# Attention steps with a gated FFN: rest-row scores by column group, dummy products removed, and the turn of a first k fill moved into the next step

## The chip, the cores and the metric

The kernel runs on one core of a Trainium2 chip. The metric is device time in microseconds (us) of one execution; the kernel before has a median of 2300.26 us over three runs (2291.55 to 2302.47). Profiles are of one further execution each, and their times are counted from its first instruction.

TensorE (PE in the profile, its weight loads PEld) multiplies, VectorE (DVE) and ScalarE (ACT) copy and compute, GpSimd (POOL) copies and issues DMAs, and SyncE (SP) issues most of the loads. Each engine works through its instructions in the order in which they were written.

## The reference

```python
g = sigmoid((x * gate_w).sum(-1, keepdims=True))          # x: 2048 x 1024
# A: attention over segments of 32 rows; 8 memory rows pass from one segment to the next
for s in range(64):
    h = concat([mem, x[32*s:32*s+32]])                    # 40 rows x 1024
    q, k, v = (h @ W for W in (Wq, Wk, Wv))               # 32 heads of 128
    p = softmax(where(mask, q @ k.T * 128**-0.5, -1e9))   # mask: i < 8 or i >= j
    o = (p @ v) @ Wo
    mem, out[s] = o[:8], o[8:]
# B: a gated FFN of 3584, independent of A
b = gelu(x @ w_gate) * (x @ w_up) @ w_down
return g * a + (1 - g) * b
```

The 64 segments of A depend on each other through `mem` alone: 8 rows out of one step are inputs of the next. Rows and weights are bf16.

## The kernel before

**Stages.** A short start transposes x and writes it out in a layout for the steps (`xq_scr`, `xr_scr`). Then come 64 attention steps, which take up the time from about 0.1 to 1.66 ms. A projection of the remaining outputs and the FFN follow; the change does not touch them.

**Rows of a step.** Of a segment's 40 rows, a step computes on the path from memory to memory only 32: its first 24 x rows and the 8 memory rows (`NR = 24`). The last 8 x rows of a segment, the "rest" (`NB = 8`), depend on no memory in their q, k and v. Those of four segments together (32 rows, `hR`) are projected in advance in a "fill", one matrix (q, k or v) and one half of the heads at a time. `FILL` says which fills a step carries: one or two, by the step's number modulo 4: (k1, q1), (v0, q0), (v1), (k0). The first fill of a step (`f1`) runs in bank A1 in the second half of the step, the second (`f2`, in steps 0 and 1 of 4) in bank B0 at the beginning of the next step.

**What happens with a fill.** `fill_evac` (L856) lets ScalarE copy the bank into a stage buffer. For v, four POOL DMAs write it to DRAM from there. For q and k, `fill_put` (L867) follows: a "turn" (TensorE transposes four 128x128 blocks into PSUM bank TT, L673), a VectorE copy back into the same buffer in a new order (L873), and a POOL DMA to `qk_scr` (L876) on the DMA lane `fq`. A lane has one semaphore, and each DMA of a lane waits until the one before has landed. Steps four and more later read these rows back (`load_qk`, L536).

The stage buffer of a first fill is `kS`. It lies in the memory of `kT` and is also the buffer into which ScalarE copies each step's own k of the first half of the heads (`evac`, L656), ahead of that k's turn. The planner of the program (`_Prog`) derives all waits from such overlaps: a write waits for every earlier reader of the same bytes, DMAs included.

**Order.** The program is written as a walk over weight pieces: 8 pieces for each matrix and half of the heads. A step's walk is: four pieces of k (round 0), two of q, the last four of the previous step's output projection, two of q, four of v, then the rest of k, q and v of round 0, then round 1 of k, q, the output projection, v, and four more of the output projection. `plan(s)` hangs all other work on a place in this walk: `on("k", 0, 2, f)` runs f ahead of the third k piece. Within an engine that order stands.

**Between two steps.** When the first four pieces of the last output projection are through (L804), `fold(s, 0)` (L815, L816) adds the halves on VectorE into `a_bf`. `next_mem(s, 0)` has TensorE transpose it (L825) and VectorE copy the 8 memory rows into `hT` of the next step (L828), and the first k piece (L771) reads that. Where the step has a second fill, four of its pieces stand before L825 and four behind it. Where it has none, `warm` (L851) issues five and two rounds of four products of 32x512 whose result nobody reads. `fill_put` of a first fill stands ahead of the fold, at `("o", 1, 3)` (L983).

**Scores.** For a half of the heads, 16 heads lie in a 4x4 grid (j, g): g chooses a 32-row group of PSUM, j a place in its columns. `scores` makes, for every (j, g), one product of 32 query rows and one of the 8 rest rows with the 40 keys (L700), into columns 80j and 80j + 40. A mask (`mS`, L687) is added by a product beforehand. The softmax (L706 to L714) works on all 128 rows at once; its result `pAB` is transposed in blocks of 32x32 by two VectorE instructions of 256 columns (L720). `attend` multiplies with v: L729 waits for the first of the two, L737 for the second.

**Queues.** SP issues the weight loads as slots come free: a freed pair of k pieces lets SP issue the next k load (L431), and so on. POOL issues, in its order, the loads of rest rows (L536, L540), the fills' writes (L862, L876) and each step's `a_scr` write (L1004), with its own copies in between (L754, L880).

Of the kernel before, what the change touches and what calls it, by code (L numbers as in the profile page):

```python
# [8 lines left out]
ALU = mybir.AluOpType  # L9
# [201 lines left out]
def bass_gated_mix__memory_aug_recurrent_mem_tr__geglu_ffn__prompt_kernel(  # L211
# [21 lines left out]
    NB = SEG - NR  # L233
# [12 lines left out]
    with ExitStack() as es:  # L246
# [218 lines left out]
        for g in range(4):  # L465
            q = slice(32 * g, 32 * g + 32)


            pw(mS, lambda e, q=q: sel(e, mS[q, 0:NR], ALU.is_ge, NEG, 0, [[-1, NR]], 1))
            pw(mS, lambda e, q=q: sel(e, mS[q, 32:40], ALU.is_ge, NEG, -NR, [[0, NB]], 1))  # L470

            pw(mS, lambda e, q=q: sel(e, mS[q, 72:80], ALU.is_ge, NEG, 0, [[-1, NB]], 1))
# [15 lines left out]

        def tr_mem(e):
            for kc in range(KC):  # L490
                ins = e.transpose(PBV[5][:, kc * 8:(kc + 1) * 8], pm[0:8, kc * 128:(kc + 1) * 128], ident[0:8, 0:8])
            return ins
# [62 lines left out]
        op("pe", tr_mem, rd=[pm.r(), ident.r()], wr=[BK(5)])  # L555
# [135 lines left out]
        def scores(u, masked=True):  # L691
# [3 lines left out]
            def f(e):  # L695
                for n, c in ((32, 0), (8, 40)):
                    for j in range(4):
                        for g in range(4):
                            x = 8 * (4 * j + g)
                            ins = e.matmul(PB[SS][32 * g:32 * g + n, j * 80 + c:j * 80 + c + LQ],  # L700
                                           lhsT=qT[:, j, g, :] if n == 32 else qkr[:, 2 * u, x:x + 8],
                                           rhs=kT[:, j, g, :], start=False, stop=True, skip_group_check=True)
                return ins
# [15 lines left out]
            for c in (0, 256):  # L719
                op("dve", lambda e, c=c: e.transpose(tAB[:, c:c + 256], pAB[:, c:c + 256]), rd=[pAB.r(c, c + 256)], wr=[tAB.r(c, c + 256)], after=[fin])  # L720
# [126 lines left out]
        def warm(n):  # L847
            def f(e):
                for x in range(4 * n):
                    g = x % 4  # L850
                    ins = e.matmul(PB[B0][32 * g:32 * g + 32, :], lhsT=hR[:, 7, :], rhs=spare[:, g * 512:(g + 1) * 512],  # L851
                                   start=True, stop=True)
                return ins
            spare = slots[home["q", 0, 7]]
            op("pe", f, rd=[hR.r(224), spare.r()], wr=[BK(B0)])

# [11 lines left out]
        def fill_put(m, u, G, st, bank=TT):  # L868
            if m == "v":
                return  # L870
            st = stage[st]
            turn(st, bank)
            op("dve", lambda e: e.tensor_copy(st[:, :].rearrange("p (i x c) -> p x i c", i=4, x=16),  # L873
                                              PBV[bank][:, 0:512].rearrange("p (x i c) -> p x i c", x=16, i=4)), rd=[BK(bank)], wr=[st.r()])
            m4 = 3 * u if m == "q" else 1 + u
            op("pool", lambda e: e.dma_start(qk_scr[:, 4 * G:4 * G + 4, m4, :], st[:, :].rearrange("p (i y) -> p i y", i=4)),  # L876
               rd=[st.r()], wr=[("D", "qk", G, m, u)], lane="fq")
# [22 lines left out]
        def plan(s):  # L900
# [80 lines left out]
            if fl:  # L981
                on("o", 1, 0, lambda: fill_evac(*fl[0], A1, "k"))
                on("o", 1, 3, lambda: fill_put(*fl[0], "k"))  # L983
# [10 lines left out]
            on("k", 0, 0, some(f2, 4) if two else lambda: warm(5), **nx)  # L994
            on("k", 0, 0, lambda: next_mem(s, 0), **nx)
            on("k", 0, 0, some(f2, 4) if two else lambda: warm(2), **nx)
            if two:
                on("k", 0, 0, lambda: fill_evac(*fl[1], B0, ua), **nx)
# [177 lines left out]
```

## Time and profile before

| what | value |
|---|---|
| median of 3 runs | 2300.26 us |
| the profiled execution | 2308.1 us, its span 2306.3 us |
| TensorE busy over the span | 2119.9 us, 92% |
| VectorE, ScalarE, GpSimd busy | 1028.8, 541.4, 423.7 us |
| products of the steps' projections (L771) | 12288, 778.4 us busy |
| products of fills (L841) | 3072, 225.3 us busy |
| dummy products (L851) | 924, 64.6 us busy |
| scores (L700), 32 rows and 8 rows | 2048 each, 37.1 and 37.4 us busy |
| transposes (L720) | 256 of 256 columns, 98.7 us busy |
| DMA, mean over the span | 277 GB/s, of which q1 (SP) 596.58 MB of 638.34 |

How to read it: "busy" of TensorE counts modelled ends of pipelined products, so four products into four column groups overlap, and a set of four of 512 columns takes about 0.217 us of TensorE's time. The line of 40 slices has 57.7 us a slice; the steps lie in slices 3 to 28. In the timeline a row has start, length, engine, line, operation, operands and count; in brackets stands the idle time ahead of it and what ended it. A DMA's row is the time of its issue only; its landing is in another view. PEclk is the clock that was granted to TensorE, in tenths.

### The profile page before, as it was taken

Reading aid. Unit: us, or ns where it says so; the run is one execution under the profiler, and the core shown is the slowest. Engines: PE = TensorE matmul, PEld = TensorE weight load, DVE = VectorE, ACT = ScalarE, POOL = GpSimd, SP = SyncE. Lnnn points to the kernel's source line nnn. Section 1 sums busy time; section 2 is a strip of 40 time slices with the busy share of each in tenths; the row PEclk is TensorE's granted clock in tenths of the full one; section 3 lists DMA queues with packets and bytes.
Section 4 is the critical chain, followed back from the end, with each engine's and each line's share of the span. In section 5 each row is a group of like instructions: output and inputs, shape, how many; then the busy total and the mean of one; then the engine's idle time right before and its main releaser. Section 6 shows DMA issues by size and latency. Waiting matters only on the chain.

```text
span 2306.3 us, 74586 instructions
## 1 busy us (share of the span) xinstructions
PE 2119.9 (92%) x33852; PEld 1048.7 (45%) x33852; DVE 1028.8 (45%) x2440; ACT 541.4 (23%) x1111; POOL 423.7 (18%) x821
## 2 busy tenths in 40 slices
PE   4598999999999999999999999998899999999999
PEld 2244444444444444444444444444464444444444
DVE  3343444454444444544444444454316446163462
ACT  1122222222222222222222222221113123032130
POOL 4422212222222222222222222221100000000000
PEclk8799999999999999999999999999899999999999
DMA  9989999898998999999989899999964440903520
GB/s 375 354 298 327 334 341 358 321 354 320 327 330 325 340 336 316 344 325 355 332 325 354 312 331 341 317 340 324 342 204 143 150 151 10 291 20 125 172 87 19
DMA packets 237579, 638.34 MB, mean 277 GB/s; under 512 B 22440, under 2 KB 91304, under 8 KB 230480
## 3 DMA queue, kind: packets, MB, share of 16 engines
q1 hardware_dynamic: 213440, 596.58, 72.4%
q0 software_dynamic: 13888, 26.31, 3.5%
q10 hardware_dynamic: 9936, 10.69, 1.4%
q8 instruction: 266, 4.36, 0.8%
q14 instruction: 49, 0.40, 0.0%
HBM read 596.85 MB, written 36.63 MB: 275 GB/s over the span
## 4 chain that ended last, share of the span: by engine, by line
PE 70%; DMA 19%; issue 4%; DVE 4%; ACT 2%; POOL 1%; ACTq 0%; SPq 0%; POOLq 0%
PE pb L771 23%; PE pb L1077 15%; DMA sl<-in_A_Wv_dram 7%; PE pb L1131 5%; PE pb L841 5%; PE pb L804 4%; PE pb L787 4%; PE pb L673 3%; DMA qkr<-qk_scr 3%; PE pb L1027 3%; PE pb L1112 2%; PE pb L851 2%; DMA wall<-wg_scr 2%; DMA xr_scr<-xr 1%; DMA o_scr<-oRc 1%
## 5 line engine op out<-in xcount | busy, mean ns | idle before, releaser
L771 PE MATMUL pb<-sl,hT 128*32 128x512 bf16 x12288 | 778.4, 383 | 28.8 <-issue 16.9
L771 PEld LDWEIGHTS pb<-sl,hT 128*32 128x32 bf16 x12288 | 337.5, 97 | 331.6 <-issue 50.8
L841 PE MATMUL pb<-sl,hR 128*32 128x512 bf16 x3072 | 225.3, 392 | 4.1 <-issue 3.2
L1077 PE MATMUL pb<-xT,wg 128*128 128x512 bf16 x896 | 211.7, 379 | 0.7
L1077 PE MATMUL pb<-xT,wu 128*128 128x512 bf16 x896 | 211.7, 379 | 0.0
L804 PE MATMUL pb<-wall,oT 128*32 128x256 bf16 x4056 | 150.9, 275 | 22.9 <-issue 8.5
L787 PE MATMUL pb<-wall,oT 128*32 128x512 bf16 x2048 | 152.4, 387 | 17.1 <-issue 9.5
L656 ACT ACTIVATE kS<-pb 128x512 bf16<-128x512 f32 x127 | 75.8, 597 | 384.3 <-PE pb L771 364.9
L815 DVE COPY part<-pb 64x256 f32<-64x256 f32 x128 | 54.0, 422 | 247.9 <-PE pb L804 246.9
L754 POOL COPY oRc<-oT 128x128 bf16<-128x128 bf16 x128 | 96.4, 753 | 359.2 <-DVE oT L659 357.0
L1131 PE MATMUL pb<-wd,GT 128*128 128x512 bf16 x672 | 146.0, 379 | 1.7 <-DMA wd<-in_B_w_down_dram 1.7
L1085 ACT ACTIVATE s<-pb 128x512 f32<-128x512 f32 x112 | 66.8, 596 | 311.9 <-PE pb L1077 311.9
L708 ACT ACTIVATE E<-pb 128x320 bf16<-128x320 f32 x128 | 55.9, 437 | 352.9 <-DVE pb L707 352.9
L1077 PEld LDWEIGHTS pb<-xT,wg 128*128 128x128 bf16 x896 | 87.2, 98 | 108.0 <-DVE GT L1093 3.7
L1077 PEld LDWEIGHTS pb<-xT,wu 128*128 128x128 bf16 x896 | 87.7, 98 | 105.7
L804 PEld LDWEIGHTS pb<-wall,oT 128*32 128x32 bf16 x4056 | 100.6, 96 | 74.9 <-ACT oT L656 25.9
L1086 DVE SCALAR_TENSOR_TENSOR tp<-s,pb 128x512 f32<-128x512 f32 x112 | 77.0, 687 | 124.2 <-ACT s L1085 124.0
L659 DVE CAST oT<-pb 128x160 bf16<-128x160 f32 x256 | 76.5, 320 | 111.7 <-PE pb L737 111.7
L659 DVE COPY kT<-pb 128x512 bf16<-128x512 bf16 x128 | 54.4, 425 | 159.8 <-PE pb L673 159.5
L880 POOL COPY kT<-qkr 128x128 bf16<-128x128 bf16 x128 | 37.3, 291 | 466.3 <-DVE kT L659 222.6
L841 PEld LDWEIGHTS pb<-sl,hR 128*32 128x32 bf16 x3072 | 82.3, 98 | 70.7 <-issue 20.8
L1090 DVE SCALAR_TENSOR_TENSOR tp<-tp,pb 128x512 f32<-128x512 f32 x112 | 77.1, 688 | 78.6 <-ACT tp L1089 78.6
(100 smaller groups left out, 2286.8 us busy)
## 6 DMA issues: line engine op xcount, KB each, us to landing
sl<-in_A_Wv_dram SPq DMA_DIRECT2D x128, 1024.0 KB, 10.8
wall<-wg_scr SPq DMA_DIRECT2D x53, 1536.0 KB, 9.2
sl<-in_A_Wk_dram SPq DMA_DIRECT2D x64, 1024.0 KB, 5.9
sl<-in_A_Wq_dram SPq DMA_DIRECT2D x64, 1024.0 KB, 9.0
wall<-wo_scr SPq DMA_DIRECT2D x120, 512.0 KB, 6.0
wd<-in_B_w_down_dram SPq DMA_DIRECT2D x42, 1024.0 KB, 5.4
sl<-in_A_Wv_dram SPq DMA_DIRECT2D x75, 512.0 KB, 11.1
wall<-in_A_Wo_dram SPq DMA_DIRECT2D x41, 512.0 KB, 7.9
```

The lines of the kernel that those rows point to most:

```text
L656: op("act", lambda e: e.activation(o, i, ACTF.Copy), rd=rd, wr=wr)
L659: op("dve", lambda e: e.tensor_copy(o, i), rd=rd, wr=wr, after=after)
L673: ins = e.transpose(PBV[bank][:, j * 128:(j + 1) * 128], st[:, j * 128:(j + 1) * 128], ident[:, :])
L754: op("pool", lambda e: e.tensor_copy(oRc[:, :, 16 * u:16 * u + 16].rearrange("p c x -> p x c"), oT[:, :, :, 32:40].rearrange("p g j c -> p ...
L771: ins = e.matmul(PB[bk][32 * g:32 * g + 32, :], lhsT=h[:, i, :], rhs=w[:, g * 512:(g + 1) * 512], start=(n == 0), stop=(n == 7))
L787: ins = e.matmul(PB[XO][32 * g:32 * g + 32, :], lhsT=oT[:, j, x, 0:32], rhs=wall[:, na:nb + 1:nb - na, c:c + 256], start=(n == 0 and hp == 0),
L804: ins = e.matmul(PB[XO][32 * g:32 * g + 32, 256 * b:256 * b + 256], lhsT=oT[:, j, x, 0:32], rhs=w[:, c:c + 256], start=False, stop=(n % 4 ...
L841: ins = e.matmul(PB[b][32 * g:32 * g + 32, :], lhsT=h[:, k[2], :], rhs=w[:, g * 512:(g + 1) * 512], start=(n == 0), stop=(n == 7))
L1077: ins = e.matmul(PB[bk][:, 0:FB], lhsT=w[:, kc, cc:cc + 128], rhs=xT[:, :, :, kc, :].rearrange("p t i c -> p (t i) c"), start=(kc == 0), s ...
L1086: op("dve", lambda e, hg=hg, t=t: e.scalar_tensor_tensor(out=t[:, :], in0=s1[:, :], scalar=1.0, in1=hg, op0=ALU.add, op1=ALU.mult), rd=[BK ...
L1090: op("dve", lambda e, hu=hu, t=t: e.scalar_tensor_tensor(out=t[:, :], in0=t[:, :], scalar=1.0, in1=hu, op0=ALU.add, op1=ALU.mult), rd=[BK( ...
L1131: ins = e.matmul(PB[bank[2 * k + hf]][:, :], lhsT=GT[:, j, tb * 128:(tb + 1) * 128], rhs=w[:, jj, hf * 512:(hf + 1) * 512], start=(j == 0) ...
```

## The change

Four things change.

1. The 8 rest rows of the four heads of a column group are multiplied together: per group g one product of 32 rows (8 for each j) with the keys of all four j, 160 columns. Of the four blocks of each row only the one with its own j is used. For this the q rows are stored g before j (in `fill_put`). The mask for the rest keys (columns 72 to 79 of `mS`) is now needed for all 32 rows of a group; it is made once at the start from a small tile `mT`, through a TensorE transpose. 
2. The transposes of `pAB` become four of 128 columns: first the rest blocks of both halves, placed 56 columns apart, so that head j's 8 rest columns come to lie at 64j + 32; then the main blocks, which overwrite what is unused. Each of the latter waits for the rest transpose of its half.
3. `warm` goes, with both its calls.
4. `fill_put` of a first fill moves from `("o", 1, 3)` of its step, ahead of the fold, to `("k", 0, 2)` of the next step, behind L825 and two k pieces.

```diff
-            pw(mS, lambda e, q=q: sel(e, mS[q, 72:80], ALU.is_ge, NEG, 0, [[-1, NB]], 1))
...
+        mT = al("mT", [128, 16, NB])
+        pw(mT, lambda e: e.memset(mT[0:NB, :, :], 0.0), True)
+        pw(mT, lambda e: sel(e, mT[0:NB, :, :], ALU.is_ge, NEG, 0, [[0, 16], [1, NB]], -1))
...
+            e.transpose(PBV[5][:, 64:64 + NB], mT[0:NB, :, :].rearrange("p x i -> p (x i)"), ident[0:NB, 0:NB])
...
+        op("dve", lambda e: e.tensor_copy(mS[:, 72:80], PBV[5][:, 64:64 + NB]), rd=[BK(5)], wr=[mS.r(72, 80)])
...
-                for n, c in ((32, 0), (8, 40)):
-                    for j in range(4):
-                        for g in range(4):
-                            x = 8 * (4 * j + g)
-                            ins = e.matmul(PB[SS][32 * g:32 * g + n, j * 80 + c:j * 80 + c + LQ],
-                                           lhsT=qT[:, j, g, :] if n == 32 else qkr[:, 2 * u, x:x + 8],
-                                           rhs=kT[:, j, g, :], start=False, stop=True, skip_group_check=True)
+                for j in range(4):
+                    for g in range(4):
+                        ins = e.matmul(PB[SS][32 * g:32 * g + 32, j * 80:j * 80 + LQ], lhsT=qT[:, j, g, :],
+                                       rhs=kT[:, j, g, :], start=False, stop=True, skip_group_check=True)
+                for g in range(4):
+                    ins = e.matmul(PB[SS][32 * g:32 * g + 32, 0:320].rearrange("p (j c) -> p j c", j=4)[:, :, LQ:80],
+                                   lhsT=qkr[:, 2 * u, 32 * g:32 * g + 32],
+                                   rhs=kT[:, :, g, :], start=False, stop=True, skip_group_check=True)
...
-            for c in (0, 256):
-                op("dve", lambda e, c=c: e.transpose(tAB[:, c:c + 256], pAB[:, c:c + 256]), rd=[pAB.r(c, c + 256)], wr=[tAB.r(c, c + 256)], after=[fin])
+            def halves(k, w, after):
+                return [op("dve", lambda e, c=c: e.transpose(tAB[:, c + 32 * k:c + 32 * k + 4 * w].rearrange("p (j x) -> p j x", j=4)[:, :, 0:32],
+                                                             pAB[:, c:c + 256].rearrange("p (j k x) -> p j k x", j=4, k=2)[:, :, k, :]),
+                           rd=[pAB.r(c, c + 256)], wr=[tAB.r(c, c + 256)], after=[x]) for c, x in zip((0, 256), after)]
+            halves(0, 64, halves(1, 56, [fin, fin]))
...
-            op("dve", lambda e: e.tensor_copy(st[:, :].rearrange("p (i x c) -> p x i c", i=4, x=16),
-                                              PBV[bank][:, 0:512].rearrange("p (x i c) -> p x i c", x=16, i=4)), rd=[BK(bank)], wr=[st.r()])
+            to = st[:, :].rearrange("p (i g j c) -> p j g i c", i=4, g=4, j=4) if m == "q" else st[:, :].rearrange("p (i j g c) -> p j g i c", i=4, j=4, g=4)
+            op("dve", lambda e: e.tensor_copy(to, PBV[bank][:, 0:512].rearrange("p (j g i c) -> p j g i c", j=4, g=4, i=4)), rd=[BK(bank)], wr=[st.r()])
...
-                on("o", 1, 3, lambda: fill_put(*fl[0], "k"))
+                on("k", 0, 2, lambda: fill_put(*fl[0], "k"), s=s + 1)
...
-            on("k", 0, 0, some(f2, 4) if two else lambda: warm(5), **nx)
+            if two:
+                on("k", 0, 0, some(f2, 4), **nx)
             on("k", 0, 0, lambda: next_mem(s, 0), **nx)
-            on("k", 0, 0, some(f2, 4) if two else lambda: warm(2), **nx)
             if two:
+                on("k", 0, 0, some(f2, 4), **nx)
                 on("k", 0, 0, lambda: fill_evac(*fl[1], B0, ua), **nx)
```

More of the change, by code (lines that the diff above doesn't have):

```diff
@@ L554, in bass_gated_mix__memory_aug_recurrent_mem_tr__geglu_ffn__prompt_kernel @@
                 load_x(n + 3)
-        op("pe", tr_mem, rd=[pm.r(), ident.r()], wr=[BK(5)])
+        op("pe", tr_mem, rd=[pm.r(), mT.r(), ident.r()], wr=[BK(5)])
+        op("dve", lambda e: e.tensor_copy(mS[:, 72:80], PBV[5][:, 64:64 + NB]), rd=[BK(5)], wr=[mS.r(72, 80)])
         op("dve", lambda e: e.tensor_copy(memT[:, :], PBV[5][:, 0:64]), rd=[BK(5)], wr=[memT.r()])
@@ L845, in fill @@
             return out
[L847 to L855, printed above, removed]
         def fill_evac(m, u, G, b, st):
```

## The prediction

> **What bounds the kernel now.** I read the page first, then the groups of instructions by form, the waits, the timeline of two neighbouring steps, and the DMA issues of short stretches.
>
> ```profile
> PE 2119.9 (92%) x33852; PEld 1048.7 (45%) x33852; DVE 1028.8 (45%) x2440; ACT 541.4 (23%) x1111; POOL 423.7 (18%) x821
> ...
> PEclk8799999999999999999999999999899999999999
> DMA  9989999898998999999989899999964440903520
> ```
>
> Attention (slices 3 to 28) keeps both TensorE and the DMA engines nine tenths busy. Its 63 step periods, measured from one first transpose of `a_bf` (L825) to the next step's, average 24.3 us. On the timeline TensorE issues with few gaps. The idle gaps of over 60 ns between 130 and 1640 us sum to 105.5 us, of which 54.5 us (74 gaps) are "issue" and 22 us end with a weight landing. So TensorE sets the pace and DMA is close behind. DMA has one thin stretch a step, just after L825, when the loads in flight have landed and no slot is free. The windows around one step show it (stretch, length, the busy time of PE, PEld, DVE, ACT and POOL, clock, DMA share, GB/s): the share falls from 0.98 to 0.64, and is 0.93 again in the next.
>
> ```profile
> 884.50:887.80 3.30, 3.28 (x85) 1.68 (x78) 1.82 (x5) 1.09 (x3) 1.71 (x3) 1.00 0.98 402
> 887.80:890.90 3.10, 2.90 (x63) 1.73 (x67) 0.17 (x1) 0.00 (x0) 0.07 (x1) 1.00 0.64 162
> ```
>
> Around that stretch lies what the change moves. On the timeline this step's L825 stands at 887.77 and its first L771 at 888.37; the next step's, which has two fills, at 912.80 and 913.83.
>
> ```profile
> 885.94 0.40 PE L673 MATMUL pb<-ident,kS 128*128 128x128 bf16 x4
> ...
> 887.09 0.78 POOL L876 DMA_DIRECT2D qk_scr<-kS  x1 [0.67 <-DVE kS L873]
> ...
> 889.02 0.38 SPq L431 DMA_DIRECT2D sl<-in_A_Wk_dram  x1
> ...
> 893.90 0.60 ACT L656 ACTIVATE kS<-pb 128x512 bf16<-128x512 f32 x1 [8.02 <-PE pb L771]
> ...
> 894.64 0.40 PE L673 MATMUL pb<-ident,kS 128*128 128x128 bf16 x4
> ```
>
> The reader is to see one buffer, `kS`, used twice. The fill's turn (885.94) leads to a DMA that reads `kS` (887.09). Then ScalarE overwrites it with this step's k (893.90), and TensorE waits for that copy before the k turn (894.64).
>
> **The change part by part.** Phases below count from a step's L825.
>
> *The moved turn.* Of the first fills only those of k are turned, so 29 turns move (31 issues of `qk_scr<-kS` less two at the start). Each takes TensorE turn, VectorE copy and POOL's DMA along. From turn to issue is 887.09 − 885.94 = 1.15 us. The new place is after 8 k products: 0.60 + 0.43 + 0.1 (change of weights), so the turn starts near 1.1 and the DMA is issued near 2.2. With two fills L771 starts at 1.03, so it is issued near 2.7. Before, it was issued at −0.67 in both. ScalarE's copy into `kS` must wait until this DMA has landed, and TensorE stands in order behind it. What is the landing time at phase 2.2 to 2.7? No `qk_scr` DMA was issued there. The nearest POOL issues are these, each a line of another answer on a short stretch (size, then us to landing):
>
> ```profile
> qk_scr<-kS POOLq DMA_DIRECT2D x1, 128.0 KB, 3.5
> vB<-v_scr POOLq DMA_DIRECT2D x1, 64.0 KB, 6.5
> vB<-v_scr POOLq DMA_DIRECT2D x1, 64.0 KB, 5.8
> qk_scr<-0S POOLq DMA_DIRECT2D x1, 128.0 KB, 6.6
> ```
>
> The first is today's, at phase −0.67 (median over all 31: 3.8). The second and third are the only two vB loads issued as late as phase 2.2 to 2.3, after SP's Wk load had started the new burst; the fourth is at phase 5.1. A DMA issued before Wk lands in 2 to 4 us, one behind it in 5.8 to 6.9. I take 6.2 (nearest in phase); ends 3.9 and 6.8.
>
> The k turn then starts 0.05 + 0.74 after the landing (893.90 to 894.64 is 0.74): at 2.2 + 6.2 + 0.8 = 9.2, and 9.7 with two fills. Undisturbed, the mean phases of that turn (27 steps of the timeline) are 6.66 and 7.41, plus 0.44 for the fill's turn now ahead of it: 7.1 and 7.85. The stall is 2.1 and 1.85 us; I take 1.9 x 29 = **+55 us**. At 3.9 it is 0, at 6.8 about 2.5 x 29 = +72.
>
> POOL: behind the moved put stand the second fill's put (steps with two fills), which shares lane `fq` and must await the k put's landing (8.9 instead of its 5.1), a_scr, and the first `kT<-qkr` copy. That copy follows the k turn's VectorE copy, itself delayed to 10.1, so it finds POOL free. That second put lands near 15 instead of 12; its reader is ScalarE's k1 copy, then delayed to about 14, and the turn behind it to about 15.9, so it hides behind the first stall. Of SP's queue only the Wq load and those after it are issued 0.4 later.
>
> What leaves the old place: VectorE's copy stood ahead of L815. L815 starts 0.16 after the last L804 product in these steps and 0.05 in the others: −0.11 x 29 = **−3**. The 0.33 of the turn itself is paid in either place. Late weights gain time during the stall: of the 22 us of landing waits and 9 us on late ScalarE copies, 29/63 lie in these steps, and I take half: **−8** (ends 0 and −14).
>
> *Scores.* One block has 16 products 128x40 and 16 of 8 rows, 0.11 us each set; after, 4 products of 160 columns replace the second set. A 512-column set of four takes 0.217, so 160 columns 0.07 at least: 0.03 x 64 second blocks = **−2**. In the first block VectorE decides.
>
> *Transposes.* Two of 256 columns end 0.445 and 0.77 after they start.
>
> ```profile
> L720 DVE STREAM_TRANSPOSE tAB<-pAB x256: 401/424/447, 92.5 to 1650.2; 128x256 bf16<-128x256 bf16 x128
> ```
>
> In the first block L737 starts 0.058 after the second transpose's end, at the median: it is bound by it. The second follows the first by 0.325. L712 (256 columns, 425 ns) and L714 (64 columns, 219 ns) give 1.07 ns a column, so 0.275 for 256, and 0.05 is fixed. Four of half the columns cost two more: +0.10 x 63 = **+6**. At worst each waits for the one before: 4 x (0.31 + 0.034) − 0.77 = +0.6, +38 us; at best 0. The second block has 0.3 us or more of slack at L729, which hides it.
>
> *Dummy products.* 231 sets of four go (924 products, 64.6 us busy). They filled the fold's wait: L825 starts 0.057 after a_bf with fills and 0.084 with dummies; the first L771 is also awaiting hT. 31 x about 0.06 = **−2**.
>
> *Instructions.* 924 + 127 x 12 = 2448 of 33852 products go, 7.2%. If the "issue" gaps shrink alike: **−4**. The start-up changes (mT on POOL, one transpose, one small copy) are under 1 us and replace four selects.
>
> *Clock.* TensorE has eight idle gaps between 1.88 and 2.5 us in slices 3 to 28, and four of them were followed by 3.4 us at a granted 0.50. One of these, and the window behind it:
>
> ```profile
> 685.93 0.59 PE L787 MATMUL pb<-wall,oT 128*32 128x512 bf16 x5 [1.88 <-issue]
> 687.00:690.40 3.40, 3.40 (x64) 1.45 (x68) 2.13 (x6) 0.44 (x1) 0.97 (x2) 0.50 0.75 213
> ```
>
> Half clock for 3.4 us costs 1.7. For stalls about 1.9 long I take a quarter of 29: 7 x 1.7 = +12. Where the dummies stood, 1.1 + 0.45 us idle leaves a 3.4 us stretch 55% busy; the stretches that lost the clock were at most 48% busy. One or two of 31 with another wait beside: +2. Sum **+14**.
>
> Sum: 55 − 3 − 8 − 2 + 6 − 2 − 4 + 14 = +56. The profiled execution took 2308.1 us (span 2306.3), 7.8 over the median of 2300.26. So 2364 on its scale, **2356 us** on the median's.
>
> **Pages against rows.** The Trainium skill, "DMA: Bandwidth & Descriptors", section "Anatomy of one DMA — SWDGE (gpsimd) path", fits a GpSimd-issued DMA with 2.0 us plus its bytes over 436 GB/s. For 128 KB that is an estimate of 2.3 us, so no stall and rival A's time. The trace agrees only in the thin stretch, where vB landed in 2.1 at the least; the 6.5 and 5.8 above speak against it. The Trainium skill, "TensorE: Matmul & The Clock Gate", section "HAM oscillation — how this bites in real kernels", puts the loss of clock at idle gaps over about 3.4 us. By that the clock would stay, rival B's time. The 1.88 us gap above, followed by 0.50, disagrees.
>
> **Rivals.**
> - A, the put lands in time, as at its old place. The limit is 4.1 us (7.1 − 0.8 − 2.2), or 4.35 with two fills. For it: a median of 3.8. Against: the vB rows. Time: no 55, no −8, clock +2: 2308.1 − 3 − 2 + 6 − 2 − 4 + 2 = 2305, 2297 on the median's scale.
> - B, the stall comes but the clock stays: four of the eight gaps kept it. 56 − 14 = +42, 2342.
> - C, the clock is lost at nearly every stall, as at the two first (2.46 and 2.48 us): 29 x 1.7 = 49 instead of 12, +93, 2393.
> - D, faster: TensorE's instruction supply. "Issue" is its largest cause of idle time (54.5 us). If 2448 products and as many weight loads fewer end half of these gaps (−27 rather than −4), it is 23 us below A: 2274. The point from which it decides is the landing: beyond about 5 us the stall (29 us for each us) outweighs it. Against: instruction fetches come in equal blocks (266 packets, 4.36 MB), so the gaps should fall with their number, by a fourteenth.
>
> **How the numbers follow.** My forecast 0.60, B 0.13, C 0.09, A 0.12, D 0.06. A measurement here tells 0.5% (11.5 us) from no change. The forecast, B and C are slower, A mostly same: slower 0.84, same 0.09, faster 0.07. The range goes from A's 2297 to a little over C's 2393, where the 6.8 us landing (+17) and worse transposes also lie: 2296 to 2400. The likeliest case's own range is 2330 to 2385.
>
> **What will show it.** Right: `qk_scr<-kS` lands in about 6 us; a new wait of ScalarE's kS copy on it, some 55 us or more in total, and of the k turn behind it; four transposes ending 0.87 after they start instead of 0.77; some 8 more windows at 0.50; steps without a k put as long as before. Wrong: kS landing in 4 us or less (A), or transposes costing 0.4 more and L737 late in all steps.

## The result, and the profile after

The changed kernel takes 2393.14 us at the median (2383.28 to 2396.66) beside 2301.36 us of the kernel before: a ratio of 1.0396, with a 95% interval of 1.037 to 1.0422. That is 92 us slower. The prediction was 2356, in a range of 2296 to 2400. Its direction holds, and its size is short by 37 us.

The profiled execution of the changed kernel has a span of 2392.7 us, 86.4 more than before. The first fence is the page of the changed kernel: busy times, the granted clock and the DMA share by slices, and the shares of the chain that ended last.

```profile
PE 2097.4 (88%) x31393; PEld 996.2 (42%) x31393; DVE 1043.8 (44%) x2697; ACT 538.5 (23%) x1111; POOL 423.7 (18%) x819
...
PEclk8699999999999999999999999999999999999999
DMA  9989999898898988899898898989976160622530
...
PE 55%; DMA 33%; DVE 5%; ACT 3%; issue 3%; POOL 1%; ACTq 0%; SPq 0%; POOLq 0%
```

TensorE is 22.5 us less busy (the dummy products are gone) in a span that is 86 us longer, so it waits 109 us more. In the chain of before TensorE had 70% and DMA 19%; now DMA has 33%. By the clock line nothing seems lost, because a slice of 60 us hides windows of 3.4 us.

All of it lies between the steps' first transposes of `a_bf`: the 62 periods between them (not 63) sum to 1506.6 us before and 1595.0 after, +88.4. Below, "one fill" and "two fills" are the two kinds of step whose beginning now holds a fill's k turn, without and with a second fill behind it. Their mean periods rise from 23.97 to 26.12 and from 24.30 to 28.00 us. The two other kinds stay (24.47 to 24.63, 24.44 to 24.07). Here is one step with two fills on the timeline of the changed kernel, cut to the rows that matter (start, length, engine, line, tiles, idle time before it and what ended that).

```profile
954.46 0.23 PE L834 MATMUL pb<-ident,a_bf 64*128 64x64 bf16 x2
...
956.03 0.40 PE L678 MATMUL pb<-ident,kS 128*128 128x128 bf16 x4
...
956.14 0.38 SPq L431 DMA_DIRECT2D sl<-in_A_Wk_dram  x1
...
957.18 0.77 POOL L875 DMA_DIRECT2D qk_scr<-kS  x1 [3.49 <-DVE kS L873]
...
964.30 0.60 ACT L661 ACTIVATE kS<-pb 128x512 bf16<-128x512 f32 x1 [6.27 <-DMA qk_scr<-kS]
...
964.76 0.76 POOL L875 DMA_DIRECT2D qk_scr<-0S  x1 [6.81 <-DMA qk_scr<-kS]
...
964.96 0.40 PE L678 MATMUL pb<-ident,kS 128*128 128x128 bf16 x4 [2.82 <-ACT kS L661]
...
971.50 0.60 ACT L661 ACTIVATE 0S<-pb 128x512 bf16<-128x512 f32 x1 [2.48 <-DMA qk_scr<-0S]
```

Read it as three links (a "put" is the DMA of `fill_put`, the "k turn" the turn of the step's own k). The fill's turn (956.03) leads to a put at 957.18, one microsecond behind the new Wk load. ScalarE's copy over `kS` waits until the put has landed, and TensorE's k turn waits for that copy: 2.82 us idle. POOL's second put, on the same lane, also waits for that landing; it goes out at 964.76, phase 10.3 instead of 5.1, and lands so late that the copy of k1 over `0S` (971.50) waits for it in turn. The stretches of the same step (length, busy time of PE, PEld, DVE, ACT and POOL, granted clock, DMA share, GB/s) show the stall, and the window that begins 1.6 us behind its end:

```profile
961.91:964.96 3.05, 0.23 (x8) 0.01 (x1) 0.00 (x0) 0.66 (x2) 0.20 (x1) 1.00 1.03 373
966.53:969.94 3.41, 3.41 (x56) 1.60 (x56) 2.26 (x7) 0.93 (x2) 0.78 (x2) 0.50 0.99 357
```

The waits of the whole execution (total, times, longest) name the same links:

```profile
ACT kS L661 <- DMA qk_scr<-kS: 231.6, 28, 12.3
...
POOL qk_scr L875 <- DMA qk_scr<-kS: 115.2, 17, 8.3
...
PE pb L678 <- ACT kS L661: 94.3, 35, 5.9
...
ACT 0S L661 <- DMA qk_scr<-0S: 33.2, 13, 4.6
```

Between 130 and 1640 us, the granted clock fell to a half in 29 windows instead of 5 (31 and 6 if counted to the end of the steps). Of the 28 steps with a moved put, 17 have such a window behind the stall. The next table puts the longer steps together from means over some 14 steps of each kind (us, before and after):

| stretch of a step | one fill | | two fills | |
|---|---|---|---|---|
| first transpose of `a_bf` to the k turn | 6.66 → 9.82 | +3.16 | 7.41 → 10.54 | +3.13 |
| k turn to attention's first product (L729, now L738) | 5.80 → 6.68 | +0.88 | 5.77 → 6.67 | +0.90 |
| from there to the turn of k1 | 0.39 → 0.32 | −0.07 | 0.34 → 1.20 | +0.86 |
| from there to the next step | 11.16 → 9.55 | −1.61 | 10.50 → 9.76 | −0.74 |

The first row holds the stall and the 0.33 to 0.44 us of the fill's own turn, the second the half clock, the third the second put. The second row is a mean of two cases: 7.29 us in the 17 steps with a window at half clock, 5.73 in the 11 without. The last row gives some back, and not because of the stall: a version without the stall ("The wait, or the place", below) has 9.89 and 9.76 us there too. It is the old place of the turn that is gone from this row.

### The profile page after: what moved, and what is told of

Read it like the earlier page. It is cut to its first block, busy times and chain, and to the rows that moved or that the text cites. A ratio compares the mean times of both kernels' runs of the same rounds, so it can differ in the third digit from the quotient of the medians.

```text
span 2392.7 us, 69920 instructions
## 1 busy us (share of the span) xinstructions
PE 2097.4 (88%) x31393; PEld 996.2 (42%) x31393; DVE 1043.8 (44%) x2697; ACT 538.5 (23%) x1111; POOL 423.7 (18%) x819
## 4 chain that ended last, share of the span: by engine, by line
PE 55%; DMA 33%; DVE 5%; ACT 3%; issue 3%; POOL 1%; ACTq 0%; SPq 0%; POOLq 0%
PE pb L780 16%; PE pb L1077 14%; DMA qk_scr<-kS 9%; PE pb L1131 6%; DMA wall<-wg_scr 5%; PE pb L796 4%; PE pb L678 3%; DMA qkr<-qk_scr 3%; DMA wall<-wo_scr 3%; PE pb L850 3%; DMA sl<-in_A_Wv_dram 2%; PE pb L813 2%; PE pb L1027 2%; PE pb L1112 2%; DMA qk_scr<-0S 2%
## 5 line engine op out<-in xcount | busy, mean ns | idle before, releaser
L780 PE MATMUL pb<-sl,hT 128*32 128x512 bf16 x12288 | 800.6, 394 | 25.4 <-DMA sl<-in_A_Wv_dram 10.1
L780 PEld LDWEIGHTS pb<-sl,hT 128*32 128x32 bf16 x12288 | 312.9, 99 | 354.6 <-issue 50.9
L850 PE MATMUL pb<-sl,hR 128*32 128x512 bf16 x3072 | 218.5, 391 | 1.9 <-issue 1.3
L678 PE MATMUL pb<-ident,kS 128*128 128x128 bf16 x384 | 41.4, 235 | 94.3 <-ACT kS L661 94.3
L726 DVE STREAM_TRANSPOSE tAB<-pAB 128x128 bf16<-128x128 bf16 x512 | 114.0, 280 | 4.4
```

Source lines behind the costliest of these rows:

```text
L678: ins = e.transpose(PBV[bank][:, j * 128:(j + 1) * 128], st[:, j * 128:(j + 1) * 128], ident[:, :])
L726: return [op("dve", lambda e, c=c: e.transpose(tAB[:, c + 32 * k:c + 32 * k + 4 * w].rearrange("p (j x) -> p j x", j=4)[:, :, 0:32], pAB[: ...
L780: ins = e.matmul(PB[bk][32 * g:32 * g + 32, :], lhsT=h[:, i, :], rhs=w[:, g * 512:(g + 1) * 512], start=(n == 0), stop=(n == 7))
L850: ins = e.matmul(PB[b][32 * g:32 * g + 32, :], lhsT=h[:, k[2], :], rhs=w[:, g * 512:(g + 1) * 512], start=(n == 0), stop=(n == 7))
```

## The experiments

Ratios are to the kernel before, with 95% intervals. Half-clock windows are counted between 130 and 1640 us. Where dummy products are in a kernel, their result is read by nothing, and the output is the same.

### The turn alone, and all but the turn

The changed kernel with the turn back at its old place:

```
-                on("k", 0, 2, lambda: fill_put(*fl[0], "k"), s=s + 1)
+                on("o", 1, 3, lambda: fill_put(*fl[0], "k"))
```

> The changed kernel with the turn of the first k fill at its old place (ahead of the fold); dummies stay out, scores and transposes stay new. If the moved turn's DMA, which holds kS against ScalarE's copy, is the cause, nearly all of the loss goes: 2290 to 2315 us (new transposes +6 to +10, the rest about 0 or a little below). If the loss came from the dummies (clock) or from VectorE's longer chain in the scores, it stays at 2340 us or more. In the profile: no wait of the kS copy on qk_scr<-kS; half-clock windows tell whether the dummies mattered (2 to 6 if not).

Measured: 2303.31 us, ratio 1.0022 (1.0005 to 1.0038). The other way round, the kernel before with this one line of the change:

```
-                on("o", 1, 3, lambda: fill_put(*fl[0], "k"))
+                on("k", 0, 2, lambda: fill_put(*fl[0], "k"), s=s + 1)
```

> The kernel before with the moved turn alone (dummies in, old scores). If the moved turn is the cause: 2380 to 2405 us, and the wait of the kS copy on qk_scr<-kS of some 230 us as in the changed kernel. If another part is: 2295 to 2310 us. Set beside e1 it tells whether the parts add up, and whether the issue gaps of TensorE (54.5 us before, 4.4 us after) vanish with the turn or with the fewer instructions.

Measured: 2374.26 us, ratio 1.0326 (1.0306 to 1.0346), which is 6 us below the band expected. So the loss goes with the moved turn. It is worth 73 us in the old kernel (2374.26 − 2301.09, the median of before beside it) and 90 (2393.14 − 2303.31) with the rest of the change; the difference comes back further down.

### The wait, or the place

If the loss is the wait for the put, a put that holds nothing up on the way to the k turn must cost nothing. Here the turn stays where the change has it, but the copy behind it goes into the buffer of `oT`, once the output projection has read that, and the DMA leaves from there, at phase 5.0 (one fill) or 5.5 (two fills) instead of 2.2 or 2.7. The second put has its own lane.

```
-                on("k", 0, 2, lambda: fill_put(*fl[0], "k"), s=s + 1)
+                on("k", 0, 2, lambda: turn(stage["k"]) if fl[0][0] != "v" else None, s=s + 1)
...
+            if fl:
+                on("q", 0, 2, lambda: fill_put(*fl[0], "k", by="o"), **nx)
...
-                on("q", 0, 2, lambda: fill_put(*fl[1], ua, SS), **nx)
+                on("q", 0, 2, lambda: fill_put(*fl[1], ua, SS, "fq2"), **nx)
```

> The changed kernel with the moved turn where it is, but its VectorE copy and its DMA go through another buffer, the stage on oT, once the o products have read it (issued near phase 4.5 to 5), and the second put has a lane of its own. The DMA still lands late (6 to 7 us), but nothing of this step's k waits for it any more. If the loss is the wait of ScalarE's kS copy for the put, and what follows from it, the k turn starts at 7.1 to 7.9 again and the time is 2295 to 2315. If the loss lies in the moved turn itself, in its VectorE copy on the path, or in the load that the late put adds to the DMA engines, it stays above 2340.

Measured: 2301.95 us, ratio 1.0007 (0.9991 to 1.0023). The k turn starts at 7.28 (one fill) and 7.89 us (two fills) instead of 9.82 and 10.54. Of ScalarE's waits in this kernel, these two matter. The copy over `kS` waits for TensorE's products, as in the kernel before, and the put now holds another copy, that of v:

```profile
ACT kS L661 <- PE pb L780: 367.3, 61, 12.4
...
ACT vA L661 <- DMA qk_scr<-oS: 44.3, 28, 2.4
```

The put itself lands as late as ever (the line on its source, which holds all of the fills' puts; the moved ones alone have medians of 7.3 and 7.2 us):

```profile
DMA to landing us min/median/max: 5.0/7.2/8.5
```

A landing 7.2 us after the issue costs next to nothing here, for TensorE waits for that copy of v only 6.1 us in all. The place of the turn is therefore not the price; the reuse of `kS` is. Beside the kernel with the second put's own lane alone (2374.81 us, below) this run is 73 us faster. The copy and the DMA did not stay at the change's place, so what they would cost there without the reuse is not shown. This is also the only version with the moved turn that is as fast as the kernel before, and no version tried is faster than that.

### When the put lands

The put is issued at phase 2.2 (one fill) or 2.7 (two fills) and lands in 6.8 or 6.9 us; at its old place it took 3.8. Is it the time since the step began, or the Wk load that SP issued in between? This kernel issues it earlier, right behind the transposes:

```
-                on("k", 0, 2, lambda: fill_put(*fl[0], "k"), s=s + 1)
...
             on("k", 0, 0, lambda: next_mem(s, 0), **nx)
+            if fl:
+                on("k", 0, 0, lambda: fill_put(*fl[0], "k"), **nx)
```

> The changed kernel with the moved turn one place further on its way back: right behind the transposes of a_bf, ahead of the first k products, not behind eight of them. The put is then issued near phase 1.65 instead of 2.2 (2.7 with two fills). If the price of the move is the landing of the put (it lands in 6.8 us when issued at 2.2 to 2.7, behind the new burst of weight loads, and in 3.8 at phase -0.67), the landing should fall to between 3.9 and 6.3 us and the k turn should start between 6.7 and 8.8 instead of 9.8 (kind with one fill) and 10.5 (two fills): time 2305 to 2350. If any place behind the transposes costs the same, whatever the load of the DMA engines, it stays at 2370 or more.

Measured: 2329.99 us, ratio 1.0113 (1.0077 to 1.0148). The timeline of this kernel shows a step with one fill and then one with two. The put leaves at the same phase in both, 1.65:

```profile
906.07 0.38 SPq L431 DMA_DIRECT2D sl<-in_A_Wk_dram  x1
906.24 0.78 POOL L875 DMA_DIRECT2D qk_scr<-kS  x1 [2.65 <-DVE kS L873]
...
933.01 0.77 POOL L875 DMA_DIRECT2D qk_scr<-kS  x1 [2.76 <-DVE kS L873]
933.71 0.38 SPq L431 DMA_DIRECT2D sl<-in_A_Wk_dram  x1
```

The DMA issues of the two stretches (size, us to landing), in the same order:

```profile
qk_scr<-kS POOLq DMA_DIRECT2D x1, 128.0 KB, 7.7
...
qk_scr<-kS POOLq DMA_DIRECT2D x1, 128.0 KB, 2.5
```

Over 14 steps each the medians are 6.32 and 2.54 us. What differs is that the put is 0.17 us behind the 1 MB Wk load in the first and 0.70 ahead of it in the second. The packets show where the time goes. In the first step, from 907.40 to 910.20 us only SP's queue moves anything (packets, MB, share of the 16 DMA engines):

```profile
q1 hardware_dynamic: 184, 0.75, 90.5%
```

Behind the load the put's first packet starts 4.2 us after the issue at the median, ahead of it 1.35 us. It does not wait for the load's end: Wk lands at 912.04, 1.6 us after the put's packets begin. So at one and the same phase the landing takes 6.3 or 2.5 us, and it goes with the order against SP's first load; no run changes that order alone. To be a little ahead is not enough: in one early step with one fill the put left 0.26 us ahead of Wk and took 5.88 us.

In the steps with two fills the k turn now starts at 8.20 instead of 10.54, with one fill at 8.92 instead of 9.82. Part of the loss stays there, and with two fills Wk is issued 0.67 later.

### The second put

A lane of its own for the second put, the rest of the change as it is:

```
-               rd=[st.r()], wr=[("D", "qk", G, m, u)], lane="fq")
+               rd=[st.r()], wr=[("D", "qk", G, m, u)], lane=lane)
...
-                on("q", 0, 2, lambda: fill_put(*fl[1], ua, SS), **nx)
+                on("q", 0, 2, lambda: fill_put(*fl[1], ua, SS, "fq2"), **nx)
```

> The changed kernel, with the second fill's put on a DMA lane of its own, so that POOL no longer holds it until the first put has landed. If POOL's wait on qk_scr<-kS (115 us, 17 times) is what makes ScalarE's copy into 0S late (33 us) and TensorE wait about 0.9 us behind L746 in 14 steps, that wait goes and the time falls by 8 to 20 us, to 2373 to 2385 us. If the second put is hidden behind the first stall, as predicted, 2388 to 2397 us.

Measured: 2374.81 us, ratio 1.0336 (1.0296 to 1.0376), 18 us less than the changed kernel by the medians and 14 by the ratios; the two intervals touch. The waits of POOL in this kernel no longer have the first put's landing ahead of the second put (115.2 us before, above):

```profile
POOL qk_scr L875 <- DVE 0S L873: 31.9, 15, 2.6
```

The second put is issued at phase 5.50 instead of 10.22 and lands at 12.07 instead of 17.25. The row from attention's first product to the turn of k1 goes from 1.20 back to 0.32. That is 0.88 us in each of 14 steps, 12 us; the rest of the 18 is not placed.

### The half clock

The next runs fill the stall with products so that TensorE is not idle in it. First, 12 sets of four:

```
+            if FILL[(s - 1) % 4][0][0] == "k" and s > 0 and s // 4 + 1 < NG:
+                on("v", 0, 4, lambda: warm(12))
```

> The changed kernel with twelve sets of four dummy products (about 2.6 us of TensorE) ahead of the k turn in the 29 steps in which it waits for kS; nothing waits for them. The wait itself stays as long. If the loss of clock behind the stalls costs time (29 more windows of 3.4 us at 0.50, at up to 1.7 us each), most of these windows vanish and the time falls by 20 to 45 us, to 2348 to 2373 us. If later waits absorb the half clock, the time stays at 2385 to 2397 us although the windows vanish. Where a stall is shorter than 2.6 us the dummies themselves cost some tenths.

Measured: 2385.97 us, ratio 1.0376 (1.0358 to 1.0393). The half-clock windows fall from 29 to 13, but 12 sets are too many: the k turn starts 0.38 (two fills) and 0.58 us (one fill) later than without them. The row behind it is shorter: k turn to attention takes 5.71 (two fills) and 5.80 us (one fill) instead of 6.67 and 6.68. So 8 sets (the same edit with `warm(8)`):

> The changed kernel with 8 sets of dummy products (32, whose result nothing reads) in front of the k turn, where 12 sets ended 0.4 to 0.6 us behind the point from which the turn had its data. 8 sets take 2.0 us of the 2.6 us stall, so the turn should start where it starts without them (9.8 and 10.5). If the loss of clock behind the stall costs what the rows from the k turn to L738 show (6.67 us without dummies, 5.75 with 12 sets, 0.9 x 31 steps = 28 us), the time is 2360 to 2372. If 0.6 us of idle time more brings the loss of clock back, or if it is made good later in the step, 2380 to 2395.

Measured: 2408.16 us, ratio 1.0448 (1.0412 to 1.0483), outside both bands and slower than without dummies. The rows show where. With one fill the step does what was expected: k turn at 9.77, attention 5.71 later, the whole step 25.79 instead of 26.37. With two fills the second put now takes 7.57 us to land instead of 6.82, and the turn of k1 waits for it until 19.06 instead of 18.41; the step grows from 28.17 to 29.31. Why the put lands later is not shown. To take that link out, both edits together:

> The second put on its own lane and 8 sets of dummy products (whose result nothing reads) in front of the k turn, both together. With the shared lane, the 8 sets brought the rows from the k turn to L738 back from 6.67 to 5.72 us, but in the steps with two fills the second put then landed later (7.57 us after its issue instead of 6.82) and k1's copy waited for it, so the step was 1.1 us longer, not shorter. With its own lane nothing waits for the second put. If that is the whole of it, the loss of clock is worth about 0.9 to 1.2 us in each of 29 to 31 steps here: 2375 - 28 = 2347, between 2340 and 2355. If the time that the clock gives back goes to the landings of later loads in any case, 2362 to 2378.

Measured: 2368.54 us, ratio 1.0313 (1.029 to 1.0336). That is 6 us below the own lane alone, within the intervals of both and so not clear of noise, where 28 were expected if the clock had its full price. One step of each on the timeline of TensorE, first with the own lane alone:

```profile
930.65 0.40 PE L678 MATMUL pb<-ident,kS 128*128 128x128 bf16 x4 [3.78 <-ACT kS L661]
...
932.81 5.07 PE L780 MATMUL pb<-sl,hT 128*32 128x512 bf16 x68
937.81 0.27 PE L738 MATMUL pb<-tAB,vA 32*128 32x40 bf16 x16
```

and the same step with 8 sets in front of the turn as well:

```profile
926.19 1.90 PE L860 MATMUL pb<-sl,hR 128*32 128x512 bf16 x32
929.51 0.40 PE L678 MATMUL pb<-ident,kS 128*128 128x128 bf16 x4 [1.42 <-ACT kS L661]
...
931.26 3.84 PE L780 MATMUL pb<-sl,hT 128*32 128x512 bf16 x68
935.22 0.28 PE L738 MATMUL pb<-tAB,vA 32*128 32x40 bf16 x16
```

Its stretch behind the turn ran at full clock:

```profile
929.51:932.91 3.40, 3.40 (x73) 1.75 (x77) 1.84 (x4) 0.79 (x3) 1.06 (x3) 1.00 0.98 246
```

The 68 products take 3.84 us instead of 5.07. In the means, the row from the k turn to attention gains 0.86 (two fills) and 1.09 us (one fill). But of this the step with two fills keeps 0.34 and the one with one fill 0.92, and the two kinds without a k put become 0.4 us longer each (24.02 to 24.45 and 24.03 to 24.43). TensorE's waits for landings of Wv rise from 9.0 to 21.1 us in total. So the loss of clock is real, and worth 0.9 to 1.1 us a step on the mean, but a kernel without most of it is hardly faster. The longer waits for weights are shown by the rows; that they take up the gain, and that the DMA engines are the reason, is argued from them.

Not every stall loses the clock: 17 of 28 do in the changed kernel, 20 of 28 with the own lane, 3 of 28 with the 8 sets as well. The trace tells them apart. All windows at 0.50 of a trace start a whole number of 3.413 us apart, to within 2 ns. In the changed kernel's trace, between 130 and 1640 us, 408 stretches of this grid had full clock. Of the 29 that were followed by 0.50, TensorE was at most half busy in 26; of the 379 others, in 4. So what matters is whether a stall leaves one such stretch half idle, and that depends on where it falls as well as on its length.

### The rest of the change

The dummy products alone, taken out of the kernel before (both `warm` calls replaced by nothing):

```
-            on("k", 0, 0, some(f2, 4) if two else lambda: warm(5), **nx)
+            on("k", 0, 0, some(f2, 4) if two else lambda: None, **nx)
...
-            on("k", 0, 0, some(f2, 4) if two else lambda: warm(2), **nx)
+            on("k", 0, 0, some(f2, 4) if two else lambda: None, **nx)
```

> The kernel before without its dummy products, nothing else. Costed in the prediction at -2 (shorter waits of the transposes of a_bf) and +2 (a window or two at half clock), with up to -27 if the issue gaps of TensorE depend on the number of instructions: 2297 to 2303 by the first, about 2275 by the second; 2310 or more if the fold's wait without dummies loses the clock in most of the 31 steps.

Measured: 2319.82 us, ratio 1.0072 (1.0051 to 1.0092). That lies in the band named for a lost clock, but there are only 9 half-clock windows instead of 5. In the profiled executions, the steps from which dummies went, those without a second fill, grew by 5.5 us in all, and the others, which never had dummies, by 11.7. And the new scores, transposes and stored form alone (those parts of the change's diff, in the kernel before):

```
+                for g in range(4):
+                    ins = e.matmul(PB[SS][32 * g:32 * g + 32, 0:320].rearrange("p (j c) -> p j c", j=4)[:, :, LQ:80],
+                                   lhsT=qkr[:, 2 * u, 32 * g:32 * g + 32],
+                                   rhs=kT[:, :, g, :], start=False, stop=True, skip_group_check=True)
...
+            halves(0, 64, halves(1, 56, [fin, fin]))
```

> The kernel before with the new scores, the four transposes and the new form of the stored q and k alone; the turn and the dummy products as before. The prediction has +6 for the transposes, -2 for the scores and -3 for 1524 instructions fewer: 2301 to 2306. If each transpose waits for the one before and the first block's attention is bound by them, +38: about 2339. If issue gaps go with the instructions, 2280 to 2290.

Measured: 2324.14 us, ratio 1.0067 (1.004 to 1.0094), in none of the bands. Of the 17.4 us by which its steps grew, 16.3 lie in those without a second fill, although the edit is the same in all steps. Each edit alone is slower by 0.7%, and both together (the first run above) by 0.2%. The same two edits with the moved turn complete the set:

> The changed kernel with the dummy products of before put back (their result is read by nothing): the moved turn and the new scores and transposes. The turn alone gave 2374, the turn with all the rest 2393. If the effects add up from the single runs (scores alone +15 to +22), 2390 to 2397. If it is the missing dummy products that cost the 19 us, through the clock in steps whose fold nothing covers, about 2374.

> The moved turn and no dummy products, scores and transposes as before. If the effects add up from the single runs (dummy products alone +18), 2390 to 2396. If it is the scores and transposes that cost the 19 us between the turn alone and the whole change, about 2374. If both this and the run with the scores come to 2393, the two edits do not add up, as they do not without the moved turn.

| ratio to before | neither | dummies out | new scores | both |
|---|---|---|---|---|
| turn at its old place | 1 | 1.0072 | 1.0067 | 1.0022 |
| turn moved | 1.0326 | 1.0417 | 1.0517 | 1.0396 |

The two new entries, with the moved turn, are 2394.06 us without the dummies (interval 1.0391 to 1.0443) and 2413.61 us with the new scores (1.0495 to 1.0539), the latter above all that was expected. In both rows the edits do not add up: together they cost 1.2% and 2.1% less than singly. So the 16 to 19 us (by ratios and by medians) between the turn alone and the whole change belong to no single edit. A part of the picture is seen in TensorE's waits. In the kernel with the new scores alone they are led by landings:

```profile
PE pb L780 <- DMA sl<-in_A_Wv_dram: 32.9, 36, 2.4
PE pb L703 <- POOL kT L889: 27.6, 30, 2.2
```

and in the kernel before by other things, with the same landings at:

```profile
PE pb L771 <- issue: 16.9, 20, 1.9
...
PE pb L771 <- DMA sl<-in_A_Wv_dram: 11.3, 16, 1.6
```

(`kT` of L889 is POOL's copy of the rest rows' k, which itself waits for the load of `qkr`.) TensorE's "issue" gaps between 130 and 1640 us fall from 54.5 to 15.8 us with the new scores, and to 45.5 without the dummies. That TensorE then reaches the landings earlier and waits there instead is a reading of these totals.

What the "issue" gaps are, the packets show. In the kernel before, the 60 gaps of over 0.2 us lie multiples of 127 products apart, to within one product, and each ends 1.2 to 1.6 us after a packet of 16384 bytes on the instruction queue has moved. The same holds without the dummies, with the new scores and with the whole change. So they are late blocks of TensorE's instructions, 127 products with their weight loads in each, and they stand at whatever product a block happens to begin with. A block lasts 6.32 us at the median before, 6.48 without the dummies, 6.74 with the new scores. The gaps shrink in the same order; that a longer block gives the next one time to arrive is argued from this.

Why the two edits undo each other stays open: the waits for Wv and `kT` are also higher with both (21.8 and 15.2 us of idle gaps, beside 10.6 and 7.2 before), and yet the time is 0.2% off.

## Why the prediction was right in direction and short in size

- **Moved turn** (+55): the mechanism held at every link, the put, ScalarE's copy over `kS`, the k turn. The size is the term that failed. The landing took 6.8 to 6.9 us at the median and not 6.2, the price taken by nearness in phase from the late vB loads; the upper end of 6.8 was the better row, and single puts took from 5.6 to 8.5. The k turn starts at 9.82 and 10.54 against 7.10 and 7.85 undisturbed (that is, with the fill's turn ahead of it; the kernel without the wait has 7.28 and 7.89): 2.7 us instead of 1.9, so 2.7 x 29 = 78 us. The early put shows what the landing goes with: behind Wk's issue it took 6.3 us, 0.70 us ahead of it 2.5, at the same phase.
- **Second put** ("hides behind the first stall"): refuted. It was to land near 15, its reader's turn to start near 15.9. It was issued at 10.22 instead of near 8.9, because the first put lands at 9.66 and POOL then needs about half a microsecond, and it landed at 17.25. The turn behind its reader would have stood at 17.5 without the wait (attention's first product at 17.21, and 0.32), and stood at 18.41. Own lane: −18 us. The wait on the lane was counted, but from a first landing that was too early, and with no range for the second.
- **Clock** (+14): the size was wrong and so was the currency. There were 24 more half-clock windows, not 8; 17 of 28 stalls lost the clock, not a quarter, at 1.6 us each in their row (7.29 beside 5.73). But with 15 of the windows gone only 6 us came back (2374.81 to 2368.54). Rival C (loss of clock at nearly every stall, 2393) names the time almost to the microsecond, and that is luck: 11 of 28 stalls kept the clock, and the runs do not bear out its price. With the clock at the 6 us that came back instead of 14, the stall at 78 instead of 55 and 18 for the second put, the forecast's +56 becomes +89, beside 92 measured. This sum is no proof: 78 is a row of the table, 6 and 18 are differences of runs, and terms that failed (below) still stand in it. The Trainium skill, "TensorE: Matmul & The Clock Gate", section "HAM oscillation — how this bites in real kernels", has the clock lost at idle gaps over about 3.4 us. The trace disagrees again: the stall of 2.82 us above is followed by 0.50.
- **Late weights** (−8): wrong in sign, if taken as landing waits. TensorE's gaps that end with a weight landing sum to 35.5 us after, 22.3 before (each over 60 ns, 130 to 1640 us). The last row of the table does gain 0.7 to 1.6 us a step, but so it does in the kernel without the stall: 9.89 and 9.76 us there, beside 11.22 and 10.37 with the turn at its old place and the rest of the change. So this is the **old place** (−3), which was priced too low: 1.3 and 0.6 us a step, of which the fill's turn itself is 0.33 to 0.44.
- **Instructions** (−4) and rival D: the gaps by "issue" fell from 54.5 to 4.4 us, nearly all of them and not a fourteenth. The step that failed is that they would go with the number of instruction blocks: 266 blocks became 247, but a gap is a block that comes late, and most blocks do not. D's mechanism came true and its gain did not: with the turn at its old place the gaps are 16.9 us, 38 less than before, and the kernel is 0.2% slower. In their place stand longer waits, for `a_bf`, Wv and `kT`.
- **Transposes** (+6): the four end 0.89 us after the first starts (0.87 predicted, 0.77 before), and each takes this long (the line on the source, minimum, median and maximum in ns):

```profile
L726 DVE STREAM_TRANSPOSE tAB<-pAB x512: 266/269/314, 94.8 to 1739.7; 128x128 bf16<-128x128 bf16 x171
```

- **Scores**, **dummy products**, **clock beside the fold**: with the transposes and instructions they sum to 0 in the prediction and measured 0.2% (5 us) together, but 0.7% each when made alone, which no step foresaw. TensorE's waits for `a_bf` ahead of its transposes rose from 4.1 to 32.0 us, time that the dummies had filled. The time does not follow them: without the dummies alone they are 36.8 us for +18 us of time, and with the turn at its old place and the rest of the change 38.6 us for +5.
- **Rival A** (the put lands in time) fell with the first landing. The Trainium skill, "DMA: Bandwidth & Descriptors", section "Anatomy of one DMA — SWDGE (gpsimd) path", comes near the early put 0.70 us ahead of Wk (2.54 us measured, an estimate of 2.3 by that fit). It fits neither the old place, also ahead of Wk (3.8 at the median), nor any put behind it (6.3 to 7.3).

## What to carry to other kernels

Before moving a DMA that reads a buffer, ask who writes the buffer next, and price the landing at the new place by what is ahead of it in the DMA engines: here a write of 128 KB landed in 2.5 us when it was issued 0.7 us ahead of a 1 MB load, and in 6.3 when it was 0.2 us behind it. Look at the lane too: a second transfer that must await the first inherits its delay, and can stall a place much further on. And where two limits lie close together, a local gain, such as the clock or a shorter instruction stream, has to be followed to the end of the period before it is counted.

## What the runs showed of the hardware

- A 128 KB write issued by GpSimd 0.17 us behind a 1 MB load of SyncE landed in 6.3 us at the median, and 0.70 us ahead of it in 2.5 us, at the same phase of the step. The first packet of the former moved 4.2 us after the issue, before the load had landed; that of the latter 1.35 us after it.
- The granted clock fell to 0.50 for 3.41 us after an idle gap of 2.8 us, and in the step shown the window began 1.6 us behind the end of the gap. The windows of a trace lie on one grid of 3.413 us; of those grid stretches at full clock that lost it next, 26 of 29 had TensorE at most half busy, of the others 4 of 379. 32 dummy products (1.90 us in the step shown) in the gap took most of these windows away (28 to 13 with the own lane).
- TensorE's gaps that no wait explains ("issue") fell from 54.5 to 15.8 us when 1524 products of a few columns left the scores, 4.5% of all, and to 45.5 when 924 dummy products of 512 columns left. So it is not the number alone. The gaps of over 0.2 us lie at blocks of 127 products, each 1.2 to 1.6 us behind a packet of 16384 bytes on the instruction queue. That small products use up a block sooner than the next one comes is argued, not shown (6.32 us a block before, 6.74 with the new scores).
